# A fused attention and MLP kernel: another order for the last output parts, and the last store cut into two halves of rows

## Chip, cores, metric

One core of one Trainium2 chip. The metric is the device time of one execution in microseconds (us), lower is better. A run over 1.5% above the fastest counts as slow. Where a view rounds to 0.1 us, times to 0.01 us are from the records of the same trace.

## The reference, cut to what matters

The input is 2048 rows of 640 columns in bf16. The result mixes a linear attention block and an MLP by a gate. Only the end of the MLP is touched by the parts of the change that matter:

```python
x1 = x + hs
h2 = gelu(layernorm(x1) @ w3) @ w4        # w3: 640 x 1728, w4: 1728 x 640
b  = x1 + h2
return g * a + (1 - g) * b                # g: one gate per row; a: the attention block
```

## The kernel before

Rows are worked on in four tiles of 512 rows, each of four chunks of 128 rows. For each chunk, the product with `w4` (13 matmuls over blocks of 128 of the inner dimension, and one of the remaining 64 rows) is summed in PSUM, the memory that TensorE writes to. A chunk's result is a pair of PSUM banks of 512 columns each, one `pair()` of a pool of four pairs; such a pair is one PSUM tile of the program. An eviction is the VectorE instruction that reads a finished result out of PSUM and computes the output from it. Chunks 0 and 2 are finished first. In the last tile, chunks 1 and 3 are each finished in two parts: part 1 has the last 512 columns and lies in the second bank, part 0 has the first 128 columns and lies in the first bank. I write (3,1) for part 1 of chunk 3.

```python
ps = ctx.enter_context(tc.tile_pool(name="ps", bufs=4, space=PSUM))
def pair():
    return ps.tile([P, 2, 512], F32, name="pp")
...                                                   # (cut)
for a, b in ((0, 2), (2, DC)):                        # W3, in two loads
    sp.dma_start(w3_sb[:, a:b, :], B_w3[a * P:b * P, :].rearrange("(c p) f -> p c f", p=P))
...                                                   # (cut)
def w4_dst(t, cc, pts, hf):
    n = D - TS if t == NT - 1 and cc % 2 else LT      # 128 in the odd chunks of the last tile
    return (pts[cc][:, 0, TS - n:TS], 0, n) if hf == 0 else (pts[cc][:, 1, 0:D - n], n, D)

def w4_mm(t, cc, pts, hf, start):                     # 13 matmuls
    dst, a, b = w4_dst(t, cc, pts, hf)
    for fc in range(FF):
        nc.tensor.matmul(dst, lhsT=st[t]["h2"][:, fc * TS + cc * P:fc * TS + (cc + 1) * P],
                         rhs=w4_sb[:, fc, a:b], start=start and fc == 0, stop=not start and fc == FF - 1)

def w4_part(t, cc, pts, hf):                          # eviction by VectorE, then the store
    ...                                               # (cut)
    nc.vector.scalar_tensor_tensor(oc[:, a:b], src, omg[:, c:c + 1], st[t]["x1"][cc][:, a:b],
                                   op0=ALU.mult, op1=ALU.add)
    nc.sync.dma_start(out2[c * P:(c + 1) * P, a:b], oc[:, a:b])

def w4_tile(t):
    ...                                               # (cut) chunks 0 and 2; w4_rest: the matmuls of the 64 rows
    last = t == NT - 1
    for cc, hf in ((3, 1), (1, 1), (1, 0), (3, 0)) if last else ((1, 0), (1, 1), (3, 0), (3, 1)):
        ...                                           # (cut)
        w4_mm(t, cc, pts, hf, False)
        if last:
            w4_part(t, cc, pts, hf)
```

## Time and profile before

Three runs before the prediction: 266.64, 266.78 and one slow. The profiled one took 266.17 us, with a span of 264.5 us. From the page of the kernel before, the engines (busy us, share of the span, instructions):

```profile
span 264.5 us, 4272 instructions
PE 260.0 (98%) x1744; PEld 161.5 (61%) x1744; DVE 139.5 (53%) x271; ACT 85.2 (32%) x126; POOL 21.9 (8%) x67
```

TensorE (PE) is the limit. The waits of PE in the whole run (engine, line, what it waited for: us in total, times, longest):

```profile
PE pp L484 <- DVE oc L512: 0.8, 1, 0.8
PE pp L206 <- PEq L589: 0.8, 1, 0.8
```

The second is the start of the program. The first is the only wait in it, and the timeline of the last 11 us shows where it is (start us, length us, engine, line, operation, operands, count, and in brackets the idle time before and what ended it):

```profile
253.35 1.68 DVE L500 SCALAR_TENSOR_TENSOR oc<-pp,omg,x 128x640 bf16<-128x640 f32 x2 [7.56 <-PE pp L493]
253.75 5.56 PE L484 MATMUL pp<-w_sb,h 128*128 128x512 bf16 x25
...
256.54 0.75 DVE L512 SCALAR_TENSOR_TENSOR oc<-pp,omg,x 128x512 bf16<-128x512 f32 x1 [1.51 <-PE pp L484]
257.32 5.19 SPq L514 DMA_DIRECT2D out_dram<-oc  x4
259.34 0.75 DVE L512 SCALAR_TENSOR_TENSOR oc<-pp,omg,x 128x512 bf16<-128x512 f32 x1 [2.05 <-PE pp L484]
260.15 1.61 PE L484 MATMUL pp<-w_sb,h 128*128 128x128 bf16 x26 [0.84 <-DVE oc L512]
...
261.07 0.35 DVE L512 SCALAR_TENSOR_TENSOR oc<-pp,omg,x 128x128 bf16<-128x128 f32 x1 [0.98 <-PE pp L484]
261.80 0.35 DVE L512 SCALAR_TENSOR_TENSOR oc<-pp,omg,x 128x128 bf16<-128x128 f32 x1 [0.38 <-PE pp L484]
```

Read it from the top. VectorE evicts chunks 0 and 2 while PE does the two parts of 512 columns. When (1,1) is done, its eviction runs from 259.34 to 260.09. PE does nothing until then, and then does the 26 matmuls of (1,0) and (3,0) in 1.61 us. From the start of one of them to the start of the next, which I call the pitch, is 0.056 us.

The last store, from the view of the store's line (duration of the issue in ns, min/median/max; then us from issue to landing):

```profile
L514 SPq DMA_DIRECT2D out_dram<-oc x1: 332/332/332, 262.2 to 262.2; - x1
DMA to landing us min/median/max: 1.4/1.4/1.4
```

One line of this trace turned out to be a hint that I passed over: the two loads of 64 rows in mid-kernel. One of them, in the same view (the other took 0.92 us to issue; both follow a load of 2 MB that itself took 0.57, so they are a hint and no proof):

```profile
L551 SPq DMA_DIRECT2D w_sb<-in_B_w_dram x1: 584/584/584, 102.8 to 102.8; - x1
```

### The profile page before, as it was taken

Reading aid. Unit: us, or ns where it says so; the run is one execution under the profiler, and the core shown is the slowest. Engines: PE = TensorE matmul, PEld = TensorE weight load, DVE = VectorE, ACT = ScalarE, POOL = GpSimd, SP = SyncE. Lnnn points to the kernel's source line nnn. Section 1 sums busy time; section 2 is a strip of 40 time slices with the busy share of each in tenths; the row PEclk is TensorE's granted clock in tenths of the full one; section 3 lists DMA queues with packets and bytes.
Section 4 is the critical chain, followed back from the end, with each engine's and each line's share of the span. In section 5 each row is a group of like instructions: output and inputs, shape, how many; then the busy total and the mean of one; then the engine's idle time right before and its main releaser. Section 6 shows DMA issues by size and latency. Waiting matters only on the chain.

```text
span 264.5 us, 4272 instructions
## 1 busy us (share of the span) xinstructions
PE 260.0 (98%) x1744; PEld 161.5 (61%) x1744; DVE 139.5 (53%) x271; ACT 85.2 (32%) x126; POOL 21.9 (8%) x67
## 2 busy tenths in 40 slices
PE   8999999999999999999999999999999999999994
PEld 5767555788755644555667555667565667455743
DVE  1788688899858588955403464503455313112132
ACT  1555444321165636622502212312131422233000
POOL 7100220012300140001000001000001000000000
PEclk9999999999999999999999999999999999999999
DMA  7999987055663727600132000042000041100011
GB/s 203 181 209 367 376 255 287 0 42 121 127 91 71 78 51 196 203 0 2 25 74 77 25 0 2 0 99 77 25 0 2 1 99 58 43 0 2 0 50 50
DMA packets 46285, 23.62 MB, mean 89 GB/s; under 512 B 35770, under 2 KB 45626, under 8 KB 46266
## 3 DMA queue, kind: packets, MB, share of 16 engines
q1 hardware_dynamic: 45824, 22.86, 34.7%
q10 hardware_dynamic: 442, 0.49, 0.5%
q8 instruction: 13, 0.21, 0.3%
q14 instruction: 6, 0.05, 0.1%
HBM read 12.21 MB, written 2.62 MB: 56 GB/s over the span
## 4 chain that ended last, share of the span: by engine, by line
PE 97%; ACT 1%; DVE 0%; issue 0%
PE pp L484 22%; PE pp L464 21%; PE pp L311 8%; PE pp L194 8%; PE pp L417 8%; PE pp L448 8%; PE pp L345 8%; PE pp L236 8%; PE pp L206 1%; PE pp L472 1%; PE pp L493 1%; ACT m_sb L385 1%; PE pp L364 1%; PE pp L251 0%; DVE oc L512 0%; PE pp L383 0%
## 5 line engine op out<-in xcount | busy, mean ns | idle before, releaser
L464 PE MATMUL pp<-lnxT,w_sb 128*128 128x512 bf16 x260 | 60.4, 379 | 0.0
L484 PE MATMUL pp<-w_sb,h 128*128 128x256 bf16 (+3 forms) x416 | 58.0, 299 | 0.8 <-DVE oc L512 0.8
L466 ACT ACTIVATE h<-pp 128x1024 bf16<-128x1024 f32 (+1 forms) x28 | 27.0, 963 | 82.1 <-PE pp L464 82.1
L484 PEld LDWEIGHTS <-h 128*128 128x128 bf16 x416 | 39.3, 98 | 18.8 <-issue 2.2
L464 PEld LDWEIGHTS <-w_sb 128*128 128x128 bf16 x260 | 25.4, 98 | 26.8
L500 DVE SCALAR_TENSOR_TENSOR oc<-pp,omg,x 128x640 bf16<-128x640 f32 x14 | 12.0, 881 | 41.4 <-ACT h2x L475 21.3
L451 DVE SCALAR_TENSOR_TENSOR x<-pp,gate,x 128x640 f32<-128x640 f32 x16 | 13.9, 868 | 29.4 <-PE pp L448 29.4
L420 DVE TENSOR_TENSOR x<-pp,x_sb 128x640 f32<-128x640 f32 x16 | 13.1, 820 | 22.6 <-PE pp L417 22.6
L186 ACT ACTIVATE e<-pp 128x640 bf16<-128x640 f32 (+1 forms) x26 | 21.5, 827 | 9.6 <-PE pp L236 9.6
L448 PE MATMUL pp<-m_sb,pqT 128*128 128x320 bf16 x160 | 24.3, 299 | 0.0
L417 PE MATMUL pp<-w_sb,hsT 128*128 128x320 bf16 x160 | 23.9, 299 | 0.1
L194 PE MATMUL pp<-wk_sb,xT 128*128 128x320 bf16 (+1 forms) x160 | 22.6, 300 | 0.0
L311 PE MATMUL pp<-x_sb,pk 128*128 128x320 bf16 (+1 forms) x160 | 22.3, 300 | 0.0
L236 PE MATMUL pp<-xT,hsT 128*128 128x512 bf16 x100 | 21.7, 379 | 0.0
L311 PEld LDWEIGHTS <-pk 128*128 128x128 bf16 x160 | 18.8, 117 | 3.5
L417 PEld LDWEIGHTS <-hsT 128*128 128x128 bf16 x160 | 15.6, 98 | 8.2 <-issue 0.2
L448 PEld LDWEIGHTS <-pqT 128*128 128x128 bf16 x160 | 15.7, 98 | 7.7
L194 PEld LDWEIGHTS <-xT 128*128 128x128 bf16 x160 | 15.6, 98 | 6.2 <-DMA xT<-in_A_x_dram 0.3
L345 PE MATMUL pp<-lnxT,w_sb 128*128 128x512 bf16 x80 | 17.9, 379 | 0.0
L236 PEld LDWEIGHTS <-hsT 128*128 128x128 bf16 x100 | 11.8, 118 | 9.7
L281 POOL TENSOR_SCALAR rstd<-mv 128x4 f32<-128x4 f32 (+1 forms) x11 | 3.5, 314 | 156.4 <-DVE mv L287 156.4
L188 DVE SCALAR_TENSOR_TENSOR pk<-pp,e 128x640 bf16<-128x640 f32 x16 | 13.2, 825 | 1.7
(77 smaller groups left out, 194.8 us busy)
## 6 DMA issues: line engine op xcount, KB each, us to landing
out_dram<-oc SPq DMA_DIRECT2D x14, 160.0 KB, 1.8
w_sb<-in_B_w_dram SPq DMA_DIRECT2D x1, 2080.0 KB, 10.0
w_sb<-in_B_w_dram SPq DMA_DIRECT2D x1, 1296.0 KB, 8.0
x_sb<-in_A_x_dram SPq DMA_DIRECT2D x2, 640.0 KB, 10.4
x_sb<-in_A_x_dram SPq DMA_DIRECT2D x1, 1120.0 KB, 7.9
wo_sb<-in_A_wo_dram SPq DMA_DIRECT2D x6, 160.0 KB, 6.7
w_sb<-in_B_w_dram SPq DMA_DIRECT2D x1, 864.0 KB, 5.1
hsT<-in_A_wqkv_dram SPq DMA_DIRECT2D x1, 800.0 KB, 5.4
```

The costliest lines, as they stand in the source:

```text
L186: nc.scalar.activation(ev, src, ACT.Exp)
L188: nc.vector.scalar_tensor_tensor(dst, src, 0.0, ev, op0=ALU.max, op1=ALU.add)
L194: nc.tensor.matmul(pt[:, hf, 0:n], lhsT=xT[:, dc, c * P:(c + 1) * P], rhs=wk_sb[:, dc, hf * HD:hf * HD + n], start=(dc == 0), stop=(dc == ...
L236: nc.tensor.matmul(pt[:, t % 2, :], lhsT=wq_sb[:, dc, :].rearrange("p (m j) -> p j m", j=DC)[:, j], rhs=xT[:, dc, t * TS:(t + 1) * TS], st ...
L311: nc.tensor.matmul(pt[:, hf, 0:HD + hf], lhsT=w, rhs=x_sb[:, c, hf * HD:(hf + 1) * HD + hf], start=(c == 0), stop=(c == NCH - 1))
L345: nc.tensor.matmul(pt[:, i, :], lhsT=w, rhs=lnxT[t][:, dc, :], start=(dc == 0), stop=(dc == DC - 1))
L417: nc.tensor.matmul(pt[:, hf, 0:HD], lhsT=hsT[:, fc, 2 + c * P:2 + (c + 1) * P], rhs=w2_sb[:, fc, hf * HD:(hf + 1) * HD], start=(fc == 0), ...
L448: nc.tensor.matmul(pt[:, hf, 0:HD], lhsT=pqT[:, j, c * P:(c + 1) * P], rhs=m_sb[:, j, hf * HD:(hf + 1) * HD], start=(j == 0), stop=(j == D ...
L451: nc.vector.scalar_tensor_tensor(x1, pt[:, :, 0:HD], gate[:, c:c + 1], x1, op0=ALU.mult, op1=ALU.add)
L464: nc.tensor.matmul(pt[:, k, :], lhsT=w3_sb[:, dc, fc * P:(fc + 1) * P], rhs=lnT[:, dc, :], start=(dc == 0), stop=(dc == DC - 1))
L466: nc.scalar.activation(h2[:, 2 * i * TS:(2 * i + n) * TS], pt[:].rearrange("p h e -> p (h e)")[:, 0:n * TS], ACT.Gelu_apprx_tanh)
L484: nc.tensor.matmul(dst, lhsT=st[t]["h2"][:, fc * TS + cc * P:fc * TS + (cc + 1) * P], rhs=w4_sb[:, fc, a:b], start=start and fc == 0, stop ...
```

## The change

The intent: to keep a chunk's two parts apart in time, so that PE does not wait for the eviction of the part just finished; to land the very last store sooner by giving half to a second queue; and to spare one DMA issue for `W3`.

```diff
-    for a, b in ((0, 2), (2, DC)):
-        sp.dma_start(w3_sb[:, a:b, :], B_w3[a * P:b * P, :].rearrange("(c p) f -> p c f", p=P))
+    sp.dma_start(w3_sb[:], B_w3.rearrange("(c p) f -> p c f", p=P))
@@ w4_part
-        nc.sync.dma_start(out2[c * P:(c + 1) * P, a:b], oc[:, a:b])
+        for q, r0, r1 in ((sp, 0, P // 2), (aq, P // 2, P)) if cc == 3 and hf == 0 else ((sp, 0, P),):
+            q.dma_start(out2[c * P + r0:c * P + r1, a:b], oc[r0:r1, a:b])
@@ w4_tile
-        for cc, hf in ((3, 1), (1, 1), (1, 0), (3, 0)) if last else ((1, 0), (1, 1), (3, 0), (3, 1)):
+        for cc, hf in ((1, 1), (3, 1), (1, 0), (3, 0)) if last else ((1, 0), (1, 1), (3, 0), (3, 1)):
```

Line numbers after the first hunk are one lower in the changed kernel (L483 for L484, L511 for L512), but L514 is a store's line in both.

## The prediction

> **What bounds the kernel now.** TensorE. The page's busy table has PE at 260.0 of 264.5 us (98%), and the chain that ended last is 97% PE. The waits view has only two waits of PE in the whole run: 0.83 us at the start, and 0.84 us near the end, "PE pp L484 <- DVE oc L512". Beyond that wait only the tail can be won: PE ends at 261.76, the last eviction runs 261.80 to 262.15 (0.35), the last store is issued at about 262.2 and lands 1.4 us later, the span ends at 264.5.
>
> **Why PE waits there.** In the last tile the order is (3,1), (1,1), (1,0), (3,0): two 512-column parts, then two of 128. The timeline shows the first 128-column matmul at 260.15, just after the eviction of the part before it (259.34 to 260.09). Parts (1,1) and (1,0) write different banks of one two-bank PSUM tile, yet the built program of before has the wait on that matmul. So waits go by tile, not by bank.
>
> **What the change does.**
> 1. New order (1,1), (3,1), (1,0), (3,0). Part (1,0) now needs the eviction of (1,1), over at 257.3, so it doesn't wait. But (3,0) needs the eviction of (3,1), which runs where (1,1)'s ran: 259.34 to 260.09. So the wait only moves behind (1,0). From the timeline, 26 small matmuls take 1.61 us, each 0.219: a pitch of 0.056 us, 0.72 us for 13. Part (1,0) is issued by about 259.85, before the eviction ends, so (3,0) starts at 260.15, where (1,0) started before. The gain is 13 matmuls taken into the wait: 0.72 us, all on the critical path. A gap of 0.1 to 0.3 us remains. The last eviction runs 261.07 to 261.42.
> 2. The last 32 KB store becomes two of 16 KB on two queues. Landing is 1.4 us for 32 KB and 1.7 for 128 KB in this trace, so it is mostly fixed. The Trainium skill, "DMA: Bandwidth & Descriptors", section "Rules for kernel authors", says not to bother to split into disjoint partition halves, as both spread over the same 16 engines. From the two sizes, 16 KB less is worth an estimated 0.05 us, and the second queue may cost as much. I count 0.
> 3. W3 loaded by one DMA (864 + 1296 KB before): one issue of 0.3 us less on SP at about 37 us. W3 is first used past 100 us. PE waits for no DMA there: 0.
>
> **Sum.** 266.78 - 0.72 = 266.06. The before runs scatter between 266.17 (profiled) and 266.78, which is nearly the size of the gain. Range 265.5 to 266.7.
> Chances: faster by over 2% 0.01, within 2% 0.98, slower 0.01.
>
> **What would show it.** PE's wait on L512 falls from 0.84 to 0.1-0.3 us and now stands between two 13-matmul groups; last matmul ends near 261.0; last eviction ends near 261.4; span about 263.8; two last stores land 1.3-1.4 us after issue, one on the ACT queue; nothing earlier than 253 us moves.
>
> **What would make it wrong.** If the wait does not go by tile, (3,0) has none and 0.84-1.1 us are won. If the ACT queue, unused since 3 us, issues or lands late, up to 0.5 us is given back. If the final stores queue behind (3,1)'s 128 KB, landing at about 261.8, some tenths. If a coarser W3 load delays something at 37-60 us, PE would show a DMA wait.

## The result, and the profile after

Four runs: 266.15, 266.30, 266.38 and 266.71 us, median 266.34, against a median of 266.64 for the three fast runs of the kernel before. The ratio is 0.9989, with a 95% interval from 0.9969 to 1.0008: the same within 2%, and not clear of noise. (A ratio here is the mean time of one kernel's fast runs over that of the other's fast runs of the same rounds, so not quite the ratio of the medians.) The time lies in the range that was predicted, but the gain of the medians is 0.30 us where 0.72 was expected.

From the page of the changed kernel:

```profile
span 265.0 us, 4272 instructions
PE 260.6 (98%) x1744; PEld 161.9 (61%) x1744; DVE 139.6 (53%) x271; ACT 85.1 (32%) x126; POOL 21.8 (8%) x67
```

Its waits of PE in the whole run; the one for the eviction is gone from the list, which leaves out waits under 0.15 us:

```profile
PE pp L205 <- PEq L589: 0.8, 1, 0.8
```

The timeline of its end:

```profile
253.99 1.68 DVE L499 SCALAR_TENSOR_TENSOR oc<-pp,omg,x 128x640 bf16<-128x640 f32 x2 [7.57 <-PE pp L492]
...
254.15 7.51 PE L483 MATMUL pp<-w_sb,h 128*128 128x512 bf16 x52
...
259.98 1.08 DVE L511 SCALAR_TENSOR_TENSOR oc<-pp,omg,x 128x512 bf16<-128x512 f32 x2 [2.05 <-PE pp L483]
...
261.70 0.35 DVE L511 SCALAR_TENSOR_TENSOR oc<-pp,omg,x 128x128 bf16<-128x128 f32 x1 [0.65 <-PE pp L483]
262.09 0.55 ACTq L514 DMA_DIRECT2D out_dram<-oc  x1
```

The 52 matmuls of the four parts are listed as one block, but a short wait is left in it. The chain that ended last (start us, us, what) shows that the last 13 matmuls, those of (3,0), still start only after the eviction of (3,1):

```profile
259.98 0.76 DVE oc L511
260.74 0.04 issue
260.78 0.90 PE pp L483 x13
```

The last store, in the same view as before:

```profile
L514 SPq DMA_DIRECT2D out_dram<-oc x1: 520/520/520, 262.1 to 262.1; - x1
L514 ACTq DMA_DIRECT2D out_dram<-oc x1: 551/551/551, 262.1 to 262.1; - x1
DMA to landing us min/median/max: 1.8/1.9/2.0
```

Both halves take over half again as long to issue as the whole did, and land after 1.8 and 2.0 us instead of 1.4.

The span of this profile is longer than that of before, although its time is of a faster kernel. To read through that, I cut each trace at two events: the start of the last pair of 640-column evictions (253.35 before, 253.99 after), and the end of the last eviction (262.15 and 262.05). This gives three stretches, in us, from the times in the traces:

| | start to last pair | last pair to end of last eviction | tail, to the span's end |
|---|---|---|---|
| before | 253.35 | 8.80 | 2.32 |
| after | 253.99 | 8.07 | 2.95 |
| difference | +0.64 | -0.73 | +0.63 |

The middle stretch holds the new order, the tail holds the store. The first 253 us are the same program but for the load of `W3`. Their difference arises at the start: PE's first matmuls run slower for longer in this execution, and its first long run of matmuls begins at 7.20 us instead of 6.39. Of these 0.81 us, 0.63 are left at 32 us, and that stays to the end of the stretch. Matmuls of PE between 4.8 and 7.2 us, by form (us busy, mean ns of one, idle before), first before:

```profile
L194 PE MATMUL pp<-wk_sb,xT 128*128 128x320 bf16 x7 | 2.1, 305 | 0.0
L194 PE MATMUL pp<-wk_sb,xT 128*128 128x321 bf16 x7 | 2.0, 300 | 0.0
```

and after:

```profile
L193 PE MATMUL pp<-wk_sb,xT 128*128 128x320 bf16 x5 | 2.0, 392 | 0.0
L193 PE MATMUL pp<-wk_sb,xT 128*128 128x321 bf16 x4 | 1.6, 388 | 0.0
```

The Trainium skill, "TensorE: Matmul & The Clock Gate", Part 1, says that PE starts at half its clock and is released after a window of activity that runs freely, so that the moment varies from run to run. That fits: the kernels are the same there, and both start with matmuls of 512 columns every 0.427 us, against 0.216 us near the end. Those of 320 columns follow each other every 0.137 us from about 4.9 us in one execution; in the other, every 0.267 us until about 6.5 us. The granted clock that the profile lists does not show it (1.00 in both), so this stays an inference. It is not the only source either: in eight of the 14 traces PE also waits for a load in the first 17 us, for 0.16 to 0.85 us. What the 14 traces do show is that the first stretch lies anywhere between 253.35 and 254.39 us, and that two traces of the very same kernel (the changed one, and its repeat below) are 0.39 us apart there. It is scatter, and larger than anything that the change can win. So I judge each experiment by the middle stretch and the tail, which repeat (0.01 us in the middle stretch, 0.07 us in the tail, between traces with the same code there), and use the timed ratio as a check.

### The profile page after: what moved, and what is told of

It is laid out like the page before. It is cut to its first block, busy times and chain, and to the rows that moved or that the text cites. A ratio compares the mean times of both kernels' runs of the same rounds, so it can differ in the third digit from the quotient of the medians.

```text
span 265.0 us, 4272 instructions
## 1 busy us (share of the span) xinstructions
PE 260.6 (98%) x1744; PEld 161.9 (61%) x1744; DVE 139.6 (53%) x271; ACT 85.1 (32%) x126; POOL 21.8 (8%) x67
## 4 chain that ended last, share of the span: by engine, by line
PE 97%; ACT 1%; DVE 0%; issue 0%
PE pp L483 21%; PE pp L463 21%; PE pp L193 8%; PE pp L310 8%; PE pp L416 8%; PE pp L447 8%; PE pp L344 8%; PE pp L235 8%; PE pp L205 2%; PE pp L471 1%; PE pp L492 1%; ACT m_sb L384 1%; PE pp L363 1%; PE pp L250 0%; DVE oc L511 0%; PE pp L382 0%
## 5 line engine op out<-in xcount | busy, mean ns | idle before, releaser
L483 PE MATMUL pp<-w_sb,h 128*128 128x256 bf16 (+3 forms) x416 | 58.0, 299 | 0.1
L483 PEld LDWEIGHTS <-h 128*128 128x128 bf16 x416 | 39.3, 98 | 18.0 <-issue 1.3
L193 PE MATMUL pp<-wk_sb,xT 128*128 128x320 bf16 (+1 forms) x160 | 23.2, 305 | 0.0
L186 DVE TENSOR_SCALAR e<-e 128x640 bf16<-128x640 bf16 (+1 forms) x26 | 9.5, 367 | 8.8 <-ACT e L185 7.2
```

Source lines behind the costliest of these rows:

```text
L193: nc.tensor.matmul(pt[:, hf, 0:n], lhsT=xT[:, dc, c * P:(c + 1) * P], rhs=wk_sb[:, dc, hf * HD:hf * HD + n], start=(dc == 0), stop=(dc == ...
```

## The experiments

All gave correct results. The theory at this point: the order wins 0.73 us because waits go by PSUM tile; the split store gives nearly all of it back; `W3` is worth nothing. Rivals: the order wins nothing and the rest is scatter; the store was late by chance or because it now comes closer to the 128 KB store of (3,1). For the store itself three culprits were open: two queues at the same moment, the ACT queue, or the shape of 64 rows.

The runs in one table ("order" and "last store" say what differs; medians in us; the kernel before had medians of 266.64 for the first four rows, 266.46 for the next four, 266.54 for the next two, and a single 266.44 in the last):

| run | order | last store | middle stretch | tail | median | ratio |
|---|---|---|---|---|---|---|
| e1_order_only | new | whole, SP | 8.07 | 2.31 | 266.02 | 0.9979 |
| e2_split_only | old | 64 + 64 rows, SP and ACT | 8.80 | 2.90 | 267.04 | 1.0020 |
| e4_halves_on_sp | new | 64 + 64 rows, both SP | 8.07 | 3.25 | 266.77 | 1.0010 |
| e5_whole_on_act | new | whole, ACT | 8.07 | 2.41 | 266.00 | 0.9976 |
| e3_w3_only | old | whole, SP | 8.80 | 2.38 | 266.46 | 0.9995 |
| e6_own_tile | new | whole, SP | 8.06 | 2.31 | 265.69 | 0.9970 |
| e7_column_halves | new | 64 + 64 columns, SP and ACT | 8.07 | 2.53 | 266.06 | 0.9978 |
| e9_after_again | new | 64 + 64 rows, SP and ACT | 8.07 | 2.97 | 266.41 | 1.0000 |
| e10_parts_464_176 | new, 464 + 176 columns | whole, SP | 7.85 | 2.37 | 265.65 | 0.9971 |
| e8_rows_96_32 | new | 96 + 32 rows, SP and ACT | 8.07 | 2.56 | one run, 265.85 | |
| e11_rows_80_48 | new | 80 + 48 rows, SP and ACT | 8.07 | 2.56 | one run, 266.15 | |
| e12_rows_mid_64 | new | rows 32 to 96 on SP, 0 to 32 and 96 to 128 on ACT | 8.07 | 3.00 | one run, 266.90 | |

### The order alone

```diff
# against the kernel before
-        for cc, hf in ((3, 1), (1, 1), (1, 0), (3, 0)) if last else ...
+        for cc, hf in ((1, 1), (3, 1), (1, 0), (3, 0)) if last else ...
```

> The kernel before with the new order of the four parts alone. Theory (waits go by PSUM tile; the order moves 13 matmuls into the eviction's shadow): the gap of 0.84 us in PE is gone or at most 0.15 us; from the end of the second 512-column part's matmuls to the end of the last eviction 2.1 us (before 2.85, after 2.10); the tail from the last eviction's end to the span's end as before, 2.35 us; time 0.72 us under the kernel before, ratio 0.9973, and so below the full change, which has the slower store. Rival (the order is worth nothing by itself, the measured gain is scatter of the start): the same wait stands before (3,0) and the ratio is 1.000.

Measured: ratio 0.9979 (0.9967 to 0.9992). The middle stretch is 8.07 us, the tail 2.31 us. PE's wait for the eviction is gone from the list of waits. So the order is worth 0.73 us by the trace and 0.62 us by the medians; the rival that it is worth nothing falls.

The wait has not gone entirely. In this trace the last matmul of (1,0) starts at 260.51 and the first of (3,0) at 260.84. That is 0.34 us at a pitch of 0.056, so 0.28 us are lost there. Only 0.12 us of it shows as idle time of PE, because a matmul's modelled length (0.22 us) covers the rest. (3,0) starts 0.05 us after (3,1)'s eviction ends, as (1,0) did before after (1,1)'s. The gain is that 13 of the 26 small matmuls now run beside that eviction: 13 x 0.056 = 0.73 us.

### The split store alone

```diff
# against the kernel before, w4_part
-        nc.sync.dma_start(out2[c * P:(c + 1) * P, a:b], oc[:, a:b])
+        for q, r0, r1 in ((sp, 0, P // 2), (aq, P // 2, P)) if cc == 3 and hf == 0 else ((sp, 0, P),):
+            q.dma_start(out2[c * P + r0:c * P + r1, a:b], oc[r0:r1, a:b])
```

> The kernel before with the last 32 KB store alone split into two halves of 64 rows on SP and ACT. Theory (two queues that issue at the same moment hold each other up): each issue takes 0.5 us instead of 0.33, the halves land 1.8 to 2.0 us after issue instead of 1.4, the tail after the last eviction is 2.9 us instead of 2.35, PE's wait of 0.84 us stays; time 0.5 to 0.6 us over the kernel before, ratio 1.002. Rival (the store's lateness in the profile of the full change is scatter, or comes from its being nearer to the 128 KB store): here it is 2.0 us away from that store, so tail 2.35 and ratio 1.000.

Measured: ratio 1.0020 (1.0007 to 1.0034), tail 2.90 us against 2.32, middle stretch 8.80. The lateness is there without the new order, 2.1 us away from the 128 KB store, so it is neither chance nor that neighbour. The split is a loss of about 0.6 us, by itself. Which of its properties costs that is not told by this run, and my reason for the number (two queues at one moment) turned out wrong below.

### Both halves on SP

```diff
# against the changed kernel
-        for q, r0, r1 in ((sp, 0, P // 2), (aq, P // 2, P)) if cc == 3 and hf == 0 else ((sp, 0, P),):
+        for q, r0, r1 in ((sp, 0, P // 2), (sp, P // 2, P)) if cc == 3 and hf == 0 else ((sp, 0, P),):
```

> The full change, but both halves of the last store on the SP queue, one after the other. If the lateness comes from two queues at the same moment: each half issues in 0.33 us and lands about 1.4 us after its own issue, the second is issued 0.33 us later, tail about 2.7 us. If halves of 64 rows land late by themselves: both land 1.8 us or more after issue, tail 3.0 us or more. If only the ACT queue is slow: as in the first case.

Measured: tail 3.25 us, the worst of all. The two halves in the view of their line:

```profile
L514 SPq DMA_DIRECT2D out_dram<-oc x2: 524/556/588, 262.5 to 263.1; - x2
DMA to landing us min/median/max: 1.8/1.8/1.8
```

They are one after the other on one queue, and each is still slow to issue and late to land. So it takes neither a second queue nor the same moment. The theory of colliding queues falls as the main cause; the shape of 64 rows is left.

### The whole store on ACT

```diff
# against the changed kernel
-        for q, r0, r1 in ((sp, 0, P // 2), (aq, P // 2, P)) if cc == 3 and hf == 0 else ((sp, 0, P),):
+        for q, r0, r1 in ((aq, 0, P),) if cc == 3 and hf == 0 else ((sp, 0, P),):
```

> The full change, but the last 128 columns stored whole (128 rows, 32 KB) on the ACT queue alone. If the lateness comes from two queues at the same moment: issue under 0.45 us, landing 1.4 to 1.6 us, tail 2.35 to 2.5 us. If the ACT queue, unused since the start, is slow by itself: issue 0.5 us, landing 1.8 to 2.0 us, tail 2.8 us or more.

Measured, in the view of the line:

```profile
L514 ACTq DMA_DIRECT2D out_dram<-oc x1: 354/354/354, 261.9 to 261.9; - x1
DMA to landing us min/median/max: 1.5/1.5/1.5
```

That is a landing after 1.47 us; the tail is 2.41 us, the ratio 0.9976 (0.9964 to 0.9989). The ACT queue, unused for 260 us, is at most 0.1 us worse than SP in the tail. It is not the culprit.

### The load of W3 alone

```diff
# against the kernel before
-    for a, b in ((0, 2), (2, DC)):
-        sp.dma_start(w3_sb[:, a:b, :], B_w3[a * P:b * P, :].rearrange("(c p) f -> p c f", p=P))
+    sp.dma_start(w3_sb[:], B_w3.rearrange("(c p) f -> p c f", p=P))
```

> The kernel before with W3 loaded by one DMA instead of two, nothing else. Both theories (off the path; or it is what scatters the start): if it is off the path, PE has no wait that it did not have before, the stretch from the last pair of 640-column evictions to the last eviction's end stays 8.80 us, the tail 2.32 us, ratio 1.000 within 0.0013. If it costs or wins in the start or middle, the ratio leaves 1.000 and PE shows a wait or a later first half.

Measured: ratio 0.9995 (0.9981 to 1.0009), middle stretch 8.80 us, tail 2.38 us. PE's waits are those of before and two of 0.2 us. One is for an early load of `x`, asked for long before `W3`. The other is listed without a cause, and is where the trace lacks the record of a matmul (it has 415 of that line's 416). It is off the path.

### Halves by columns

```diff
# against the changed kernel
-        for q, r0, r1 in ((sp, 0, P // 2), (aq, P // 2, P)) if cc == 3 and hf == 0 else ((sp, 0, P),):
-            q.dma_start(out2[c * P + r0:c * P + r1, a:b], oc[r0:r1, a:b])
+        for q, a0, b0 in ((sp, a, (a + b) // 2), (aq, (a + b) // 2, b)) if cc == 3 and hf == 0 else ((sp, a, b),):
+            q.dma_start(out2[c * P:(c + 1) * P, a0:b0], oc[:, a0:b0])
```

> The full change, but the last store is halved by columns: two stores of 128 rows x 64 columns on SP and ACT at the same moment. If the shape of 64 rows makes the halves late (as the two halves one after the other on SP suggest, 0.52 and 0.59 us to issue): issue 0.33 us on both, landing 1.4 to 1.5 us, tail 2.35 to 2.5 us. If two DMAs of 16 KB at once are late whatever their shape: issue 0.5 us, landing 1.8 to 2.0 us, tail 2.9 us as with the row halves.

Measured, in the view of the line:

```profile
L514 SPq DMA_DIRECT2D out_dram<-oc x1: 332/332/332, 261.6 to 261.6; - x1
L514 ACTq DMA_DIRECT2D out_dram<-oc x1: 374/374/374, 261.6 to 261.6; - x1
DMA to landing us min/median/max: 1.4/1.5/1.6
```

Again two DMAs of 16 KB on two queues at the same moment, but of 128 rows. SP's issues and lands like the whole store (1.43 us), ACT's lands after 1.59 us. The tail is 2.53 us, a little over the 2.35 to 2.5 expected. So two queues at one moment cost the second one something (1.59 against the 1.47 of the whole store alone on ACT), and win nothing for the first, although it has half the bytes. The large part of the loss goes with the rows.

### 96 + 32 rows

```diff
# against the changed kernel
-        for q, r0, r1 in ((sp, 0, P // 2), (aq, P // 2, P)) if cc == 3 and hf == 0 else ((sp, 0, P),):
+        for q, r0, r1 in ((sp, 0, 96), (aq, 96, P)) if cc == 3 and hf == 0 else ((sp, 0, P),):
```

> The full change with the last store cut into 96 rows on SP and 32 rows on ACT instead of 64 and 64. If any DMA of fewer than 128 rows issues slowly: SP's issue 0.5 us, landing 1.75 us or more, ACT's the same or later. If it goes with the number of rows by engine [...]: 96 rows near the whole store's 0.33 and 1.44 us, 32 rows slower than 64.

Measured (one look, with no state of its own):

```profile
L514 SPq DMA_DIRECT2D out_dram<-oc x1: 344/344/344, 261.6 to 261.6; - x1
L514 ACTq DMA_DIRECT2D out_dram<-oc x1: 376/376/376, 261.6 to 261.6; - x1
DMA to landing us min/median/max: 1.5/1.5/1.6
```

Both of my guesses miss. A DMA of fewer than 128 rows is not slow as such, and 32 rows are not slower than 64: this cut behaves like the column halves (1.46 and 1.62 us, tail 2.56).

### 80 + 48 rows, and 64 rows in the middle

```diff
# against the changed kernel: e11, then e12
-        for q, r0, r1 in ((sp, 0, P // 2), (aq, P // 2, P)) if cc == 3 and hf == 0 else ((sp, 0, P),):
+        for q, r0, r1 in ((sp, 0, 80), (aq, 80, P)) if cc == 3 and hf == 0 else ((sp, 0, P),):
+        for q, r0, r1 in ((sp, 32, 96), (aq, 0, 32), (aq, 96, P)) if cc == 3 and hf == 0 else ((sp, 0, P),):
```

> The full change with the last store cut into 80 rows on SP and 48 on ACT. 96 + 32 rows issued in 0.34 and 0.38 us and landed after 1.46 and 1.62 us; 64 + 64 in 0.52 and 0.56, landed after 1.76 and 2.02. If a cut near the middle is what costs (two DMAs of like size), 80 + 48 is near 64 + 64: tail 2.8 to 3.0 us. If it is DMAs of exactly 64 rows: as 96 + 32, tail 2.5 to 2.6 us.

> The full change with the last store in three: the middle 64 rows (32 to 96) on SP, rows 0 to 32 and 96 to 128 on ACT one after the other. If 64 rows as such are slow: SP's DMA issues in 0.5 us and lands 1.75 us or more after issue. If only halves that begin at row 0 or row 64 are: 0.33 to 0.38 us, landing 1.45 to 1.6 us. The two of 32 rows on ACT: about 0.38 us each, the second landing 0.4 us later than the first.

Measured (one look each): 80 + 48 rows issue in 0.344 and 0.377 us and land after 1.45 and 1.61 us, tail 2.56. The three-way cut:

```profile
L514 ACTq DMA_DIRECT2D out_dram<-oc x2: 353/394/434, 262.2 to 262.6; - x2
L514 SPq DMA_DIRECT2D out_dram<-oc x1: 600/600/600, 262.2 to 262.2; - x1
DMA to landing us min/median/max: 1.4/1.6/1.8
```

The DMA of 64 rows is slow again, 0.60 us to issue and 1.84 us to land, while the one of 32 rows that goes out on ACT at the same moment is not (0.353 us, landing 1.38 us). So among 32, 48, 64, 80, 96 and 128 rows of 256 bytes, exactly 64 rows is the slow one, wherever it begins (row 0, 32 or 64) and on either queue. The other counts below 128 were each seen in one trace only (32 in two). The three-way cut's tail of 3.00 us is not the 64-row DMA's alone: its data packets end at 263.68 us, those of the second DMA of 32 rows, whose landing isn't recorded, at 263.75.

Why 64 is special, no run here tells. But the DMA packets in the traces show where the time goes. From the start of the issue to the first packet it is 0.83 us for the whole store on SP, 0.84 for 96 and for 80 rows, and 1.17 to 1.26 for 64 rows on SP. From the first packet to the last, all of these take 0.20 to 0.25 us. So the time is lost before the data moves, not in moving it.

### The last part in a PSUM tile of its own

```diff
# against e1_order_only
 def w4_mm(t, cc, pts, hf, start):
     dst, a, b = w4_dst(t, cc, pts, hf)
+    if t == NT - 1 and (cc, hf) == (3, 0):
+        nc.tensor.matmul(dst, lhsT=st[t]["h2x"][FR:P, P:2 * P], rhs=w4_sb[FR:P, FF, a:b], start=True, stop=False)
 ...                                                  # w4_rest skips (3, 0) in the last tile
+            if last and (cc, hf) == (3, 0):
+                pts[3] = pair()
             w4_mm(t, cc, pts, hf, False)
```

> The new order with the last store whole (as in the run of the order alone), and the last part (3,0) in a PSUM tile of its own, with its matmul of the 64 remaining rows moved there. If waits go by PSUM tile: the remaining gap in PE between the two groups of 13 small matmuls, 0.28 us from issue to issue beyond the pitch, is gone, the stretch from the last pair of 640-column evictions to the last eviction's end falls from 8.07 to about 7.85 us, tail 2.31, ratio to the kernel before about 0.9965. If the gap has another cause (the order of evictions on VectorE, or the bank), it stays: 8.07 us, or 0.1 more for the extra matmul, ratio 0.9975 to 0.998.

Measured: ratio 0.9970 (0.9954 to 0.9985). The wait is gone; the time it cost is not. From the timeline:

```profile
260.30 1.08 DVE L516 SCALAR_TENSOR_TENSOR oc<-pp,omg,x 128x512 bf16<-128x512 f32 x2 [2.06 <-PE pp L486]
...
260.91 0.23 PE L484 MATMUL pp<-w_sb,h2x 64*128 64x128 bf16 x1
...
261.07 0.90 PE L486 MATMUL pp<-w_sb,h 128*128 128x128 bf16 x13
```

The first matmul into the new tile starts at 260.91, while the eviction of (3,1) runs until 261.05 (0.75 us from 260.30). In the traces with both in one tile, that start came about 0.05 us after the eviction's end. So the waits do go by tile. But the single matmul of 64 rows between matmuls of 128 is costly: the last matmul before it starts at 260.76, the first after it at 261.07, so 0.31 us go by with one matmul in them. Each of the two steps is about 0.10 us longer than the pitch (0.151 and 0.159 against 0.056). The four earlier steps in this trace from matmuls of 128 rows to those of 64 cost the same: 0.26 us, where the steps before them are 0.16. The middle stretch is 8.06 us, no better. The wait went as the theory said, the stretch stayed as the rival said, and neither had foreseen why. The Trainium skill, "TensorEngine Tiling (Array Packing)", section "Key Properties", says that changing the tiling mode drains the engine, and this trace is in keeping with it: 0.31 us for two steps that take 0.11 at the pitch. That the cost is a drain is the page's account; the trace shows only the longer steps.

The Trainium skill, "PSUM — Partial Sum Buffer", section "PSUM bank collisions raise a hardware error", says that two engines on different banks do not collide. So the wait by tile looks like the program's caution and no need of the chip: this kernel, with the matmul and the eviction in different tiles at the same time, gave a correct result. The two banks of one tile were not tried without the wait. Its median is 0.3 us under that of the order alone, but the two come from different chips, and the stretches show no such gain.

### The parts cut at 464 + 176 columns

```diff
# against e1_order_only
-        n = D - TS if t == NT - 1 and cc % 2 else LT
+        n = 176 if t == NT - 1 and cc % 2 else LT
```

> The new order with the whole store, the odd chunks of the last tile cut at 464 + 176 columns instead of 512 + 128. If the rest of PE's gap (0.28 us) is only the eviction of (3,1) outlasting the 13 small matmuls beside it, then a shorter eviction (an estimate of 0.70 us, from 0.75 for 512 and 0.35 for 128 columns) beside longer matmuls (13 x 0.076 us) leaves no gap, and the last eviction grows by 0.05 us to 0.40: the stretch from the last pair of 640-column evictions to the last eviction's end 7.84 us instead of 8.07, tail 2.3 to 2.4 us, ratio to the kernel before 0.9965. If the gap is the cost of changing tiles or of any wait that PE has to look at, it stays, and the stretch is 8.12 us or more.

Measured: ratio 0.9971 (0.9957 to 0.9985), middle stretch 7.85 us, tail 2.37 us. From the timeline:

```profile
253.67 7.24 PE L484 MATMUL pp<-w_sb,h 128*128 128x464 bf16 x52
...
258.97 0.70 DVE L512 SCALAR_TENSOR_TENSOR oc<-pp,omg,x 128x464 bf16<-128x464 f32 x1 [1.84 <-PE pp L484]
259.96 0.40 DVE L512 SCALAR_TENSOR_TENSOR oc<-pp,omg,x 128x176 bf16<-128x176 f32 x1 [0.29 <-PE pp L484]
260.95 0.40 DVE L512 SCALAR_TENSOR_TENSOR oc<-pp,omg,x 128x176 bf16<-128x176 f32 x1 [0.59 <-PE pp L484]
```

The eviction of (3,1) is over at 259.67, before (1,0) is done, and the 52 matmuls run without a gap (7.24 us for the block, against 7.51 in the changed kernel). The middle stretch was expected at 7.84. So the rest of the gap was the eviction outlasting the matmuls beside it, and nothing else. By the trace this version is 0.95 us better than the kernel before in that stretch, and 0.05 us worse in the tail. It is faster than the kernel before by 0.9 us in the medians, and its interval ends below 1; against the changed kernel, compare the repeat below, whose ratio to the kernel before is 1.0000.

### The full change again

> The full change, again, in five rounds. If the parts add up (order alone 0.9979, split alone 1.0020): ratio 0.9990 to 1.0005, stretch of the evictions 8.07 us, tail 2.95 us. If the parts interact in the whole (less loss beside the new order): ratio 0.998.

Measured, with no edit: ratio 1.0000 (0.9985 to 1.0015), median 266.41 against 266.46, middle stretch 8.07 us, tail 2.97 us. The parts add up: -0.73 and +0.65 us by the trace are -0.08, and the ratios of the order and of the split alone multiply to 0.9999. The first ratio of 0.9989 and this one agree within their intervals.

## Why the prediction was right, and where it was not

- The limit and the wait were right. PE is busy 98% of the span, and the one wait inside the program goes by PSUM tile: in e6_own_tile (3,0) starts 0.14 us before the eviction ends.
- The order: predicted 0.72 us, measured 0.73 in the trace. Also right was that the wait would not vanish but move behind (1,0); a gap of 0.1 to 0.3 us was predicted, 0.12 us shows as idle and 0.28 us is lost from issue to issue.
- `W3` in one load: predicted 0, measured none that can be told from noise (0.9995, interval from 0.9981 to 1.0009).
- The step that failed is point 2. "From the two sizes, 16 KB less is worth an estimated 0.05 us, and the second queue may cost as much. I count 0." The term measured +0.63 us in the tail of the changed kernel (2.95 against 2.32), +0.65 in the repeat and +0.58 alone. Less data was worth nothing that could be seen: 16 KB as 128 rows landed in 1.43 us, 32 KB in 1.44. What cost was a shape that I had not costed: 64 rows issue in 0.52 us instead of 0.33 and land 0.32 us later on SP (1.76 against 1.44). The half on ACT landed 0.25 us later still (2.01). The prediction had taken landing times of whole stores of 128 rows for those of halves.
- The list of risks had the size, "up to 0.5 us is given back", but blamed the ACT queue. ACT alone is fine (1.47 us).
- The Trainium skill, "DMA: Bandwidth & Descriptors", section "Rules for kernel authors", advises against splitting a transfer into disjoint partition halves. I read that as "no gain"; the measurement goes further, to a loss of 0.6 us.
- The sum, 266.06 us, was 0.28 us too low against 266.34. It started from 266.78, the middle of three runs with the slow one counted; the fast runs of the kernel before have a median of 266.64, so the base was 0.14 us too high and hid part of what was lost. The time is within the range because the range was wide for the scatter of the start, not because the sum was right: by the trace nearly all of the gain was given back. That it fell inside is in part luck: even the unchanged kernel's 266.64 us lies in that range.
- "Nothing earlier than 253 us moves" was wrong as it was put. The first stretch moved by 0.64 us in the profile, but it moves as much between profiles of any of these kernels.

## What to carry to other kernels

When PE waits for an eviction, look at which part of the same PSUM tile was finished last, put other matmuls between, and size them so that they last at least as long as the eviction: here that was worth 0.73 us by order alone and 0.95 us with the sizes matched. Cost a DMA by the duration of one of the same number of rows in your own trace, not by its bytes, and prefer one whole store at the end to two halves. When two parts of a change are of opposite sign and smaller than the scatter of the total, cut the traces at fixed events and compare the stretches.

## What the Trainium skill lacked or had wrong

- "DMA: Bandwidth & Descriptors": it has nothing on DMAs of exactly 64 rows. With 256 bytes a row, they took 0.52 to 0.60 us to issue and 1.75 to 2.02 us to land, and the first packet on SP started 1.17 us or more after the issue, against 0.83 for the whole store; 32, 48, 80, 96 and 128 rows took 0.33 to 0.43 us and, where it is recorded, 1.38 to 1.62 us. Its rule against partition halves says that they serialize; here two halves were 0.6 us worse than the whole.
- "DMA: Bandwidth & Descriptors": it says that DMAs from several issuing engines interleave on the same DMA engines and that a second one saves only issue time. It gives no cost. Here the second of two equal DMAs at the same moment landed after 1.59 us, the first after 1.43, a whole one alone on ACT after 1.47.
- "TensorEngine Tiling (Array Packing)": it says that a change of tiling mode drains the engine, without a figure. Here one matmul of 64 rows between matmuls of 128 took 0.31 us from the start before it to the start after it, two steps that take 0.11 us at the pitch: about 0.10 us for each change.
- "TensorE: Matmul & The Clock Gate": its account of a release that falls differently in each run fits the first microseconds here. It warns that clock events in a trace have been unreliable, but does not say that the profile's granted clock can read 1.00 throughout, as it did while the same matmuls took 392 ns in one run and 305 in the other.
